# A gated linear-attention and MLP-mixer kernel: fewer idle products in batch 0, more engines for small copies, and a new written-out order

## The chip, the cores and the metric

The kernel runs on one core of a Trainium2 chip. A core has five engines that work side by side, each through its own instructions in their order: TensorE (PE in the profile, its weight loads PEld) for matrix products, VectorE (DVE), ScalarE (ACT) and GpSimd (POOL) for elementwise work, and SyncE (SP), which here only issues DMA transfers. Products land in PSUM, which this kernel uses as eight banks; everything else is in SBUF. An instruction waits on semaphores for what other engines and transfers make. The metric is the device time of one execution in microseconds (us), the median of several.

## The reference

Four batches, eight heads, 768 positions, 48 channels a head. First a linear attention with a forget gate, then an MLP mixer over its output:

```
f = 1 / (1 + exp(-f_logit))
for t in range(S):
    state = f[:, :, t, :, None] * state + einsum('bhd,bhe->bhde', k[:, :, t], v[:, :, t])
    y[:, :, t] = einsum('bhd,bhde->bhe', q[:, :, t], state)
x  = y as (B, S, H*D)
h  = max(x^T @ w_tok1, 0) @ w_tok2          # over positions: 768 -> 256 -> 768
u  = x + h^T
out = u + max(u @ w_ch1, 0) @ w_ch2         # over channels: 384 -> 1536 -> 384
```

## The kernel before

**Attention.** Each batch is cut into six chunks of 128 positions. For a chunk, `gates` makes the log gate on ACT (an exp, a log) and splits it into two bf16 parts; the lower part, Llo, is a subtraction (L457). `sums_and_turns` adds the gates up along the chunk with products by a triangle (L530 and L531; in chunk 5 of batch 0 one fp32 product, L519), takes exp of the sums on ACT (GG, L541 and L543), multiplies q and k by it on DVE (qk, L562) and transposes both. In batches 0 to 2 PE transposes (L579) and the results are copied from PSUM (qkT); in batch 3 a DMA transpose on SP does it (L569). `attention` then has the scores (L476) and the chunk's part of the state (L492). `rest` masks the scores on DVE (AmT, L616), decays the state (L625 to L633), copies it, rounded to bf16, into the two halves of a block-diagonal tile (state_bd, made at L636, the copy itself at L430, L432 or L434 by engine), and forms the output of the chunk from the state (L651) and the masked scores (L658). The output is copied from PSUM to x_bf, in bf16, and to x_nat. In batches 1 to 3 the decay of a chunk travels through a small DMA (glast from ends, L556).

**Mixer.** `mixer` has for each batch the first token product (tok1, L693, 12 products), a relu (h1T), the second (tok2, L709, 12), the addition of x (L725), a rounding to u_bf (L735), a transpose to uT (PE at L750 in batches 0 and 1, a DMA transpose in 2 and 3), the first channel product (L768, 24 groups of three), 24 relus to zT (ACT at L439 or DVE at L441), the second (L787, three groups of four for each of six row blocks, the last block in two column parts), the addition (L793) and a DMA to the output (L797).

**Order.** Nothing is left to a scheduler. Every step is an `Op` with the engines it may run on, what it needs and makes, and at most one PSUM bank. `ORDER` is a tuple of 1,116 codes, one for each step: `code // 4` says which step comes next, `code % 4` which of its engines takes it. Hence each engine's instructions stand in the order of the tuple, and an engine that waits holds up all that stands behind it. `Plan.best` walks through the tuple with estimated costs. Its estimated times pick the PSUM bank of each step and the place of **idle products**: where PE is estimated free for over 250 ns before `until` (25,500 ns), it puts in products of a constant tile (`steady`, L834) that nobody reads. `cold` is the time up to which the estimate counts every PE step twice.

**Loads.** POOL issues all loads but those of batch 0's gates (ACT and SP), one at a time, on one queue: k, q and v of a chunk of batch 0, then w_tok1, the last v, w_tok2, the channel weights, and the later batches' tiles. x_nat has three buffers, so batch 3 writes into that of batch 0 once its outputs have left.

The lines on which the change bears, beside the tuple:

```
n = int((t - free[PE] - 1000) / 430) if not free[PE] else min(4, int((t - free[PE]) / 220))
...
on = (DVE, DVE, (DVE, POOL), POOL)[b]                       # Llo, by batch
...
op = add(((ACT, DVE), ACT, (ACT, POOL), POOL)[b], r, None,  # state_bd, by batch
...
op = add((ACT,) if b <= 1 else (ACT, POOL), r, None,        # u_bf
```

Of the kernel before, what the change touches and what calls it, by code (L numbers as in the profile page):

```python
# [82 lines left out]
)  # L83
KEPT = 3
SPLIT = 5
SLOTS = (5110, 5800, 7500, 8450, 9600, 10400, 11400, 13000, 14400, 14800, 16700,
         18000, 19100, 19500, 20000, 20700, 21400, 23400, 24300, 25900)
HELD = (2600, 3600, 4100, 4750, 5500, 6500)


class Op:
# [18 lines left out]
class Plan:  # L110
# [65 lines left out]
    def best(self, idle, cold, until):  # L176
# [10 lines left out]
        for code in ORDER:  # L187
            op = self.ops[code // 4]
# [65 lines left out]
def kernel(  # L254
# [581 lines left out]
    for op in plan.best(idle, 6500.0, 25500.0):  # L836
        op.fn()
# [30 lines left out]
```

## Time and profile before

| | us |
|---|---|
| median of 3 runs | 172.84 |
| lowest and highest | 172.21, 174.68 |
| the profiled execution | 171.88 |
| its span, first to last instruction | 170.2 |
| PE busy, of it | 162.9 |
| DVE busy | 128.0 |
| ACT busy | 108.2 |
| POOL busy | 99.3 |

The profile is of one execution. A row of its timeline gives the start in us from the span's start, the length, the engine, the line, the operation with what it writes and reads, and in brackets the idle time before it with what ended it. Rows of groups give the busy time, the mean length in ns, and the idle time before. The chain of waits lists, in order of time, what released what, back from the last instruction. Products overlap in PE's pipeline, and the ends that the profile gives them are modelled: a row of eight products is shorter than eight lengths, and a PE shown as busy may still have short pauses.

### The profile page before, as it was taken

The page shows a single profiled execution, that of the slowest core. Times are in us where ns is not written, and L with a number is a line of the kernel's source. Part 1 is how long each engine was busy: PE and PEld are TensorE (multiplying, and loading weights), DVE is VectorE, ACT ScalarE, POOL GpSimd, SP SyncE. Part 2 cuts the span into 40 slices and gives each one's busy share as a digit, 9 for nine tenths or more (in the row PEclk, how much of TensorE's full clock was granted, in tenths as well). Part 3 has the DMA queues.
Part 4 walks back from the last instruction along what each step waited for, and adds up shares of the span by engine and source line. Part 5 has one row for each costly group of instructions (what it writes and reads, how often), then busy time and mean ns, then how long its engine had stood idle before and what let it go on. Part 6 is the DMA issues. An engine that isn't in the chain of part 4 may idle for free.

```text
span 170.2 us, 4181 instructions
## 1 busy us (share of the span) xinstructions
PE 162.9 (96%) x1606; PEld 102.8 (60%) x1606; DVE 128.0 (75%) x287; ACT 108.2 (64%) x256; POOL 99.3 (58%) x134
## 2 busy tenths in 40 slices
PE   6899999999999999999999999999999999999992
PEld 2356565665766576665776756665666666566661
DVE  5679995966898998899999868768884723675431
ACT  4759993598879889999999978385545320510100
POOL 7999569896499969999978869603111200000000
PEclk9999999999999999999999999999999999999999
DMA  6999999999999997999998999996920060220253
GB/s 103 141 174 149 156 192 181 212 149 201 192 167 136 161 165 75 116 155 133 182 157 49 134 251 107 144 165 115 228 100 4 0 139 0 92 96 0 78 202 139
DMA packets 102547, 22.71 MB, mean 133 GB/s; under 512 B 95264, under 2 KB 101664, under 8 KB 102528
## 3 DMA queue, kind: packets, MB, share of 16 engines
q0 software_dynamic: 79440, 13.77, 101.8%
q1 hardware_dynamic: 22560, 8.59, 22.5%
q8 instruction: 12, 0.20, 0.5%
q10 hardware_dynamic: 528, 0.10, 0.3%
q14 instruction: 7, 0.06, 0.1%
HBM read 25.17 MB, written 4.72 MB: 176 GB/s over the span
## 4 chain that ended last, share of the span: by engine, by line
PE 64%; DMA 12%; DVE 7%; ACT 6%; POOL 6%; issue 2%; SPq 1%; DVEq 0%; POOLq 0%
PE ps L768 22%; PE ps L787 22%; DMA v_sb<-in_v_dram 5%; PE ps L709 4%; POOL qk_sb L360 4%; PE ps L693 4%; DMA glast<-ends 4%; DMA out_dram<-x_nat 3%; DVE AmT L616 2%; PE ps L476 2%; PE ps L579 2%; PE ps L658 2%; POOL v_sb L360 1%; PE ps L530 1%; PE ps L651 1%
## 5 line engine op out<-in xcount | busy, mean ns | idle before, releaser
L787 PE MATMUL ps<-w_ch,zT 128*128 128x384 bf16 (+2 forms) x300 | 51.6, 320 | 0.0
L768 PE MATMUL ps<-uT,w_ch 128*128 128x384 bf16 x288 | 50.6, 326 | 0.0
L439 ACT ACTIVATE zT<-ps 128x384 bf16<-128x384 f32 x56 | 25.3, 494 | 25.3 <-PE ps L768 25.2
L768 PEld LDWEIGHTS <-w_ch 128*128 128x128 bf16 x288 | 27.7, 98 | 17.7
L787 PEld LDWEIGHTS <-zT 128*128 128x128 bf16 x300 | 27.9, 98 | 16.9
L616 DVE TENSOR_TENSOR AmT<-ps,tri_bf 128x512 bf16<-128x512 f32 x46 | 30.5, 686 | 2.5 <-PE ps L476 2.3
L441 DVE TENSOR_SCALAR zT<-ps 128x384 bf16<-128x384 f32 x40 | 21.1, 554 | 8.8 <-PE ps L768 8.8
L360 POOL DMA_DIRECT2D v_sb<-in_v_dram x24 | 22.2, 925 | 4.1 <-DMA w_ch<-in_moe_w_ch_dram 4.1
L360 POOL DMA_DIRECT2D qk_sb<-in_k_dram x24 | 22.4, 932 | 0.8 <-POOLq L852 0.8
L360 POOL DMA_DIRECT2D qk_sb<-in_q_dram x24 | 22.3, 930 | 0.0
L793 DVE TENSOR_TENSOR x_nat<-x_nat,ps 128x384 f32<-128x384 f32 (+2 forms) x25 | 13.3, 535 | 10.6 <-PE ps L787 10.2
L360 POOL DMA_DIRECT2D f_sb<-in_f_logit_dram x18 | 16.5, 943 | 0.2
L562 DVE TENSOR_TENSOR qk<-qk_sb,GG 128x768 bf16<-128x768 bf16 (+1 forms) x30 | 14.2, 475 | 2.1 <-ACT GG L543 1.0
L450 ACT ACTIVATE f_sb<-f_sb 128x384 f32<-128x384 f32 x24 | 12.5, 524 | 4.6 <-DMA f_sb<-in_f_logit_dram 4.4
L434 POOL CAST state_bd<-state 48x192 bf16<-48x192 f32 x13 | 4.5, 347 | 16.2 <-DVE state L633 14.6
L725 DVE TENSOR_TENSOR x_nat<-x_nat,ps 128x384 f32<-128x384 f32 x21 | 10.5, 550 | 3.4 <-PE ps L709 3.1
L834 PE MATMUL ps<-steady 128*128 128x512 bf16 x30 | 11.3, 483 | 1.7 <-DVE steady L375 1.7
L543 ACT ACTIVATE GG<-ps 128x384 bf16<-128x384 f32 x24 | 11.6, 489 | 2.0 <-PE ps L531 1.9
L541 ACT ACTIVATE GG<-ps 128x384 bf16<-128x384 f32 x24 | 11.7, 488 | 1.4 <-PE ps L531 1.2
L579 PE MATMUL ps<-ident,qk 128*128 128x128 bf16 x144 | 11.6, 224 | 0.0
L579 PEld LDWEIGHTS <-qk 128*128 128x128 bf16 x144 | 9.2, 100 | 2.7 <-DVE qk L562 0.7
L550 ACT ACTIVATE ends<-ps 32x384 f32<-32x384 f32 x15 | 7.0, 481 | 4.9 <-PE ps L531 4.7
(81 smaller groups left out, 234.1 us busy)
## 6 DMA issues: line engine op xcount, KB each, us to landing
out_dram<-x_nat SPq DMA_DIRECT2D x23, 192.0 KB, 3.1
f_sb<-in_f_logit_dram POOLq DMA_DIRECT2D x18, 192.0 KB, 5.4
qk_sb<-in_k_dram POOLq DMA_DIRECT2D x24, 96.0 KB, 5.1
qk_sb<-in_q_dram POOLq DMA_DIRECT2D x24, 96.0 KB, 4.9
v_sb<-in_v_dram POOLq DMA_DIRECT2D x24, 96.0 KB, 5.5
w_ch<-in_moe_w_ch_dram POOLq DMA_DIRECT2D x2, 576.0 KB, 7.5
w_ch<-in_moe_w_ch_dram POOLq DMA_DIRECT2D x1, 1152.0 KB, 10.6
f_sb<-in_f_logit_dram SPq DMA_DIRECT2D x5, 192.0 KB, 4.7
```

Of the source, the lines that this page charges most:

```text
L360: lambda eng=eng, into=into, of=of: eng.dma_start(out=into, in_=of),
L439: nc.scalar.activation(out_, in_, AF.Relu, bias=0.0, scale=1.0)
L441: nc.vector.tensor_scalar(out_, in_, 0.0, None, ALU.max)
L450: add(ACT, r, lambda: nc.scalar.activation(fb, fb, AF.Exp, bias=0.0, scale=-1.0), make=[key], kind=el, need=([("fb", c)] if c < 1 else []) ...
L541: add(ACT, r, lambda: nc.scalar.activation(G[i], sview(), AF.Exp, bias=0.0, scale=-1.0), make=[("G", i)], bank=p_s, kind=el)
L543: add(ACT, r, lambda: nc.scalar.activation(Gi[i], sview(), AF.Exp, bias=0.0, scale=1.0), make=[("Gi", i)], bank=p_s, kind=el)
L562: add(DVE, r, lambda n=n: nc.vector.tensor_tensor(qk[i4][:, n, :, 0:D], qk_sb[nb][:, n, :, c, :], GG[i][:, n], ALU.mult), need=[(x, nb, c) ...
L579: nc.tensor.transpose(to[:, o + hp, :], blk(src)[:, hp, :], ident)
L616: add(DVE, r, lambda half=half, made=made: nc.vector.tensor_tensor(half, made(), tb4, ALU.mult), need=["tri_bf"], make=[("AmT", i, p)], ba ...
L768: nc.tensor.matmul(banks[pm.at][:, 0:384], lhsT=w[:, kt, c0:c0 + 128], rhs=uT[:, th, :, kt, :], start=(kt == 0), stop=(kt == 2))
L787: nc.tensor.matmul(banks[pm.at][:, 0:n1 - n0], lhsT=zT[:, kt, tt * 128:(tt + 1) * 128], rhs=w_ch2[:, kt, n0:n1], start=(kt == 0), stop=(kt ...
L793: add(DVE, rank("ch2", tt), lambda un=un, pm=pm, n=n1 - n0: nc.vector.tensor_tensor(un, un, banks[pm.at][:, 0:n], ALU.add), make=[("x_nat" ...
```

## The change

Five edits, and a new tuple:

```
-                n = int((t - free[PE] - 1000) / 430) if not free[PE] else min(4, int((t - free[PE]) / 220))
+                n = int((t - free[PE] - 1000) / 430) if not free[PE] else min(4, int((t - free[PE]) / (430 if t < cold else 220)))
...
-        on = (DVE, DVE, (DVE, POOL), POOL)[b]
+        on = (DVE, (DVE, POOL), (DVE, POOL), POOL)[b]
...
-                op = add(((ACT, DVE), ACT, (ACT, POOL), POOL)[b], r, None,
+                op = add(((ACT, DVE), (ACT, POOL, DVE), (ACT, POOL, DVE), (POOL, ACT))[b], r, None,
...
-            op = add((ACT,) if b <= 1 else (ACT, POOL), r, None,
+            op = add((ACT, POOL), r, None,
...
-    for op in plan.best(idle, 6500.0, 25500.0):
+    for op in plan.best(idle, 10000.0, 25500.0):
```

Before 10,000 ns of estimated time, not 6,500, PE steps count double, and up to there one idle product is put in for each 430 ns of estimated pause, not 220. Llo and u_bf of batch 1 may now go to POOL; state_bd may go to POOL or DVE in batches 1 and 2, and to ACT in batch 3. All 1,116 steps are the same ones, and none is added or taken away but idle products.

What the built program makes of it: 19 idle products in place of 30. Seven stand at the start as before. Until the scores of chunk 1 the order on PE (without the products by ones, which give the chunk's decay) is

```
before: 7 idle, sums 0, 1 idle, sums 1, turn q0, 2 idle, state part 0, turn k0, 4 idle, scores 0,
        3 idle, sums 2, turn 1, state part 1, turn 1, output 0, 1 idle, turn 2, 2 idle, scores 1
after:  7 idle, sums 0, sums 1, turn k0, turn q0, state part 0, turn k1, scores 0, sums 2, turn q1,
        3 idle, output 0, 1 idle, scores 1
```

and from there the other eight idle products stand in runs of 1, 1, 4 and 2, the last run between the scores of chunk 5 and the first token product. On POOL the loads keep their order up to the channel weights. On SP the output DMAs of batch 0 and the transposes of batch 3 stand in another sequence, with the transposes of chunks 4 and 5 still ahead of the last two outputs of batch 0. From the second token product of batch 0 on, the steps on PE are the same products; most groups stand within 1 us of PE work of where they stood, and some groups of the second channel product 4 to 12 us away.

The engine of a step differs in these groups:

| step | from, to | how many |
|---|---|---|
| state_bd, batch 0 | ACT to DVE 2, DVE to ACT 1 | 3 |
| state_bd, batches 1 to 3 | ACT to DVE 3, ACT to POOL 1, POOL to ACT 4 | 8 |
| x_bf and x_nat from PSUM | DVE to ACT 8, ACT to DVE 3 | 11 |
| zT | DVE to ACT 24, ACT to DVE 22 | 46 |
| u_bf, batches 2 and 3 | ACT to POOL 5, POOL to ACT 4 | 9 |
| qkT, x_bf from x_nat, u_bf and uT of batch 0, h1T | both ways | 16 |

Llo and u_bf of batch 1 stay where they were (DVE and ACT).

120 rows, old and new, of the table ORDER are left out of this document.

## The prediction

> **What bounds the kernel now.** I read the page's engine shares first, then the windows of 10 us, because the stages differ. TensorE (PE) is the engine that is never free: after the first stage each window shows it busy for 9.6 us or more of 10, while VectorE (DVE) is its only neighbour that comes close, and only up to 90 us.
>
> ```profile
> span 170.2 us, 4181 instructions
> ...
> PE 162.9 (96%) x1606; PEld 102.8 (60%) x1606; DVE 128.0 (75%) x287; ACT 108.2 (64%) x256; POOL 99.3 (58%) x134
> ```
>
> ```profile
> 10.00:20.00 10.00, 9.67 (x137) 5.68 (x135) 9.86 (x26) 7.33 (x21) 8.53 (x11) 1.00 2.36 151
> ...
> 50.00:60.00 10.00, 9.61 (x118) 6.56 (x117) 9.20 (x22) 9.08 (x22) 10.00 (x13) 1.00 2.02 154
> ...
> 80.00:90.00 10.00, 10.00 (x136) 7.15 (x134) 9.60 (x21) 9.87 (x26) 8.41 (x11) 1.00 1.86 175
> ```
>
> The columns after the length are PE, its weight loads, DVE, ACT and POOL, then the granted clock and the DMA share. But a busy PE is not a useful PE here. The windows of the idle products alone (L834) show where it only kept itself busy:
>
> ```profile
> 0.00:5.00 5.00, 3.17 (x7) 0.88 (x7) 1.00 0.93 107
> 5.00:10.00 5.00, 1.95 (x4) 0.66 (x5) 1.00 1.96 160
> 10.00:15.00 5.00, 3.03 (x10) 0.76 (x8) 1.00 2.33 155
> 15.00:20.00 5.00, 1.58 (x5) 0.45 (x5) 1.00 2.38 146
> 20.00:25.00 5.00, 1.22 (x5) 0.41 (x5) 1.00 1.61 187
> ```
>
> So some 11 us of the first 25 are idle products, and the question for the change is whether they were in the way. The chain of waits says mostly not. Batch 0 waits for what arrives:
>
> ```profile
> 11.54 8.27 DMA v_sb<-in_v_dram
> ...
> 19.85 0.31 PE ps L492 x8
> ...
> 20.81 0.80 PE ps L519 x2
> ...
> 26.56 0.20 PE ps L658 x8
> 26.76 1.16 PE ps L693 x7
> ...
> 27.94 0.50 ACT h1T L439
> ...
> 28.48 1.22 PE ps L709 x6
> ```
>
> The v chunk issued at 11.54 lands at 19.81. All later loads of batch 0 are on the same queue, and GpSimd (POOL) issues them in the same order after the change. The last v chunk and w_tok2 close the stage, and the tiles' own answers (the second view lists issues between 16 and 21 us) give their delays:
>
> ```profile
> 17.54 0.99 POOL L360 DMA_DIRECT2D v_sb<-in_v_dram  x1
> 20.09 0.70 POOL L367 DMA_DIRECT2D w_tok<-in_moe_w_tok_dram  x1 [1.57 <-DMA v_sb<-in_v_dram]
> ```
>
> ```profile
> w_tok<-in_moe_w_tok_dram POOLq DMA_DIRECT2D x2, 384.0 KB, 7.5
> v_sb<-in_v_dram POOLq DMA_DIRECT2D x2, 96.0 KB, 7.3
> ```
>
> v of chunk 5 is there at about 17.54 + 7.3 = 24.8, w_tok2 at about 20.09 + 7.5 = 27.6. Token product 2 started at 28.48. **Ceiling of the first stage: 28.48 - 27.6 = 0.9 us.**
>
> From there on the ceiling is the work itself. One pace of each kind of product, from the chain, where PE runs without a wait:
>
> ```profile
> 32.22 7.80 PE ps L768 x48
> ...
> 72.54 0.38 PE ps L750 x6
> ...
> 75.04 0.55 PE ps L476 x16
> 75.60 0.36 PE ps L492 x16
> ...
> 77.38 0.17 PE ps L530
> 77.55 0.16 PE ps L531
> ...
> 81.97 0.17 PE ps L651 x4
> 82.14 0.40 PE ps L658 x16
> ...
> 83.36 0.89 PE ps L579 x16
> ...
> 166.87 0.26 DVE x_nat L793
> ```
>
> What is left at 28.48: products of 384 columns, 288 + 288 in the channel MLP, 48 in tok2, 36 in tok1 of batches 1 to 3, together 660 at 7.80/48 = 0.1625: 107.3. Eighteen chunks' gate sums at 0.33: 5.9. Their outputs, 15 x 0.17 + 18 x 0.20: 6.2. Scores, 9 x 0.55: 5.0. State parts, 7.5 x 0.36: 2.7. q and k transposes of batches 1 and 2, 6 x 0.89: 5.3. u transposes, 36 x 0.063: 2.3. Sum 134.7. It took 166.87 - 28.48 = 138.4, so all stalls after the first stage come to about 3.7 us, though the busy column hides most of them. **No order can gain more than 0.9 + 3.7 = 4.6 us.**
>
> **The change part by part.** Idle products. The built order has 19 in place of 30; the seven at the start stay, and the other 12 stand later (first a run of 3, behind the gate sums of chunk 2). Gone are above all the seven between 6 and 11 us, six of them here:
>
> ```profile
> 8.01 1.06 PE L834 MATMUL ps<-steady 128*128 128x512 bf16 x2
> ...
> 9.74 1.50 PE L834 MATMUL ps<-steady 128*128 128x512 bf16 x4
> 11.17 0.40 PE L476 MATMUL ps<-qkT 48*128 48x128 bf16 x8
> 11.50 0.82 PE L834 MATMUL ps<-steady 128*128 128x512 bf16 x3
> ```
>
> Scores of chunk 0 (L476 at 11.17) stood behind the run of four; without it they come up to 1.5 us earlier. That is worth nothing by itself: chunk 3 waits for v at 19.81 and chunk 5's gate sums (L519) start at 20.81, both set by loads. These products also did something: four cover 1.50 us at 9.74, three 0.82 us at 11.50, so a product's pace went from about 0.4 to about 0.22 us there. The granted clock column says 1.00 on both sides and does not show it. What their absence does to that step is the slow rival below.
>
> Order at the end of batch 0. The part products of chunk 3 (L492, at 19.85 in the old order) now stand behind L519, so they move from 19.85 to about 20.81 + 0.80 + 0.37 (outputs of chunk 2) = 22.0. Behind them wait the decay on DVE and two state copies, about 0.36 + 0.66, so 23.0, for the outputs of chunk 4 (before those of chunk 5 at 26.39): covered by 3 us. What ended the stage was DVE:
>
> ```profile
> 22.81 0.55 DVE L432 COPY x_nat<-ps 128x384 f32<-128x384 f32 x1
> ...
> 24.75 1.29 DVE L616 TENSOR_TENSOR AmT<-ps,tri_bf 128x512 bf16<-128x512 f32 x2
> ```
>
> The two masks of chunk 5 end at 26.04, and its outputs follow. The new order gives the x_nat copy at 22.81 to ScalarE (ACT) and leaves the rest of DVE's row there much as it was, so the pair of 1.29 can start up to 0.55 earlier. The tok1 tail (1.16), h1T (0.50) and tok2 follow as they did. I take **-0.6**; bounds 0 (the score chain of chunk 5 still hangs on L519) and -0.9.
>
> Engine choices. Of the state copies in batches 1 to 3, three go from ACT to DVE, one from ACT to POOL and four from POOL to ACT; the roundings of batch 1 stay on ACT and its Llo on DVE, so those freedoms are unused. Over all, DVE gives ACT eight copies of PSUM outputs and takes back three.
>
> ```profile
> L430 ACT ACTIVATE state_bd<-state 48x192 bf16<-48x192 f32 x17 | 6.1, 358 | 0.6 <-DVE state L633 0.3
> ...
> L434 POOL CAST state_bd<-state 48x192 bf16<-48x192 f32 x13 | 4.5, 347 | 16.2 <-DVE state L633 14.6
> ```
>
> One copy costs 0.36 on ACT and 0.35 on POOL, so the swap is even in work. On POOL it is a wait for DVE with loads queued behind (16.2 us of idle before 13 copies); the one new POOL copy, of batch 1 chunk 2, holds a v load and the two Llo subtractions of batch 2. Its price is bounded by a swap, 0, and one decay step more in PE's way, about 0.4. Four copies fewer there free the loads and Llo of batch 3 in the same measure. I take 0 for both.
>
> Order of batches 1 to 3. In PE's order most groups move by under 1 us of PE work; the largest moves are channel products 2, which have slack. I credit a small part of the 3.7 us of stalls, **-0.3**, bounds -3.7 and +1, since DVE at 9.20 and 9.60 of 10 sets part of them and it becomes only some 2 us lighter in 128. SP: the out-DMAs of batch 0, which x_nat of batch 3 waits for, keep their place near the transposes of batch 3. Nothing credited.
>
> Sum: -0.6 - 0.3 = -0.9 against the profiled execution's 171.88 (span 170.2), so 171.0. The median of the three runs shown is 172.84, 0.96 above it; on that footing **171.9**.
>
> **The rivals.** *The array stays slow (slower).* Between 6 and 11 us PE has only the work of chunks 0 and 1, at pauses; if the step from 0.4 to 0.22 needs gapless work, it comes later, and idle products, now counted at the fast pace after 10 us, take twice as long too. PE waits again for L519 from about 18 to 20.8, with four idle products in front. If the array is slow until the u transposes of batch 0, then tok1 and tok2 (24 x 0.1625) and 18 u transposes (18 x 0.063) cost 5.0 us more, less the 0.9 gained: 172.84 + 4.1 = 176.9. If dense work from 20.8 on wakes it by 25, only a backlog of about two chunks' products stays, each near 0.45 + 0.55/2 + 0.17 + 0.20 + 0.18 = 1.3: +2.6 - 0.9, 174.5. The point that decides is whether it is fast by about 21 us. For it: PE paced slowly for 9 us although busy 5.1 of the first 10 us with idle products alone. Against: the run of three from about 11.5 on, and that chunks 0 to 2 have time to spare before 19.8. [...]
>
> *Nothing reaches the end.* DVE sets batches 1 and 2, and an earlier tok2 waits there again: 172.8. For it: 9.2 to 9.9 of 10 busy up to 90 us.
>
> *The stalls go (faster).* The new order meets most of the 3.7 us besides the first stage: -0.9 - 2.9 = -3.8, 169.0. Against it: the dense DVE windows.
>
> **The numbers.** Forecast, 170.8 to 172.8: 0.46. Nothing reaches the end: 0.12. Slow array: 0.25, 0.20 of it near its full price and 0.05 at the 174.5 of an early waking. Stalls go: 0.17, of which 0.16 at or below its price. About 2%, or 3.5 us, is what a measurement of this kernel can tell from no change: slower begins at 176.3, faster at 169.4. So faster 0.16, slower 0.20, within 0.64. The range takes in the prices of both ends, 169.0 and 176.9, which leaves out about half of each end's chance; the forecast's own range is 170.8 to 172.8.
>
> **What would show it.** Right: L834 x19; tok2 (first L709) at about 27.9; L658 of chunk 5 before 26.2; the last L787 near 166. Wrong: idle products of 0.4 us after 12 us, or L768 at over 0.2 a piece (slow array); PE idle at L530 or L651 by more than 0.5 (a new wait); the first L709 after 28.5.

## The result, and the profile after

The changed kernel takes 173.91 us (median of 21 runs, 172.86 to 179.14) against 172.48 us for the kernel before, measured beside it (21 runs, 171.03 to 176.29). The ratio is 1.0098, 95% interval 1.0077 to 1.0118: 1.7 us slower, where 0.9 us faster was forecast. Ratios, here and below, are of the executions within 1.5% of the fastest of their kernel, the times are medians of all, so a ratio need not be that of the two medians. The profiled execution took 173.56.

The page's shares, after, show an engine that did less and a span that grew:

```profile
span 171.9 us, 4146 instructions
...
PE 161.2 (94%) x1592; PEld 102.1 (59%) x1595; DVE 127.2 (74%) x284; ACT 111.5 (65%) x261; POOL 99.7 (58%) x132
```

PE is busy 1.7 us less in a span 1.7 us longer, so it idles 3.4 us more. The windows say where. After, all engines, columns as in the prediction:

```profile
0.00:10.00 10.00, 6.67 (x43) 2.92 (x43) 5.82 (x27) 5.61 (x12) 8.80 (x18) 1.00 1.48 133
...
110.00:120.00 10.00, 8.38 (x68) 5.15 (x67) 6.98 (x16) 5.51 (x13) 3.69 (x7) 1.00 1.03 159
```

The same windows before:

```profile
0.00:10.00 10.00, 7.85 (x47) 3.42 (x48) 5.56 (x28) 6.34 (x14) 8.79 (x18) 1.00 1.45 133
...
110.00:120.00 10.00, 10.00 (x106) 6.29 (x105) 7.51 (x16) 6.48 (x15) 2.24 (x5) 1.00 1.09 141
```

The 1.2 us missing in the first window are idle products left out (1.95 us of them between 5 and 10 before, none after, below), no loss by itself. The 1.6 us missing between 110 and 120 are the loss: PE was full there before. The chain of waits of after, in that stretch (start, length, what):

```profile
117.77 0.50 ACT zT L439
...
118.28 0.56 DVE qk L562
118.84 0.48 DVE zT L441
...
119.36 1.14 PE ps L768 x6
```

The channel products of batch 2 stop for PSUM: the next bank comes free with a relu (zT) on DVE, and that relu stands behind a qk product. Why the qk product is late is told by POOL's and DVE's timelines of after:

```profile
108.96 1.61 POOL L457 TENSOR_TENSOR Llo<-f_sb 128x384 bf16<-128x384 f32 x2 [3.60 <-ACT f_sb L452]
110.64 0.73 POOL L434 CAST state_bd<-state 48x192 bf16<-48x192 f32 x2
111.31 0.92 POOL L360 DMA_DIRECT2D qk_sb<-in_k_dram  x1
112.23 0.88 POOL L360 DMA_DIRECT2D qk_sb<-in_q_dram  x1
...
118.28 0.56 DVE L562 TENSOR_TENSOR qk<-qk_sb,GG 128x768 bf16<-128x768 bf16 x1 [1.92 <-ACT zT L439]
118.76 1.48 DVE L441 TENSOR_SCALAR zT<-ps 128x384 bf16<-128x384 f32 x3
```

and of before:

```profile
105.37 0.89 POOL L360 DMA_DIRECT2D qk_sb<-in_k_dram  x1
106.24 0.90 POOL L360 DMA_DIRECT2D qk_sb<-in_q_dram  x1
107.13 1.65 POOL L457 TENSOR_TENSOR Llo<-f_sb 128x384 bf16<-128x384 f32 x2
...
115.67 0.55 DVE L562 TENSOR_TENSOR qk<-qk_sb,GG 128x768 bf16<-128x768 bf16 x1
```

The last loads of k and q in the kernel, those of batch 3's chunk 5, stood ahead of two Llo subtractions on POOL. The new order puts them behind these and behind two state copies. The subtractions wait 3.60 us for ACT and take 1.61, the copies take 0.73, and q is issued 6.0 us later (112.23 against 106.24). It lands at 118.09 against 114.02. The trace names ACT as what the qk product waited for, but the product reads q and the gates, not a relu; of what it reads, q came last (118.09, and the product starts at 118.28). That the load is the cause is shown by the runs below. The page's group of channel products carries the price: 1.8 us of idle where before it had 0.0.

```profile
L768 PE MATMUL ps<-uT,w_ch 128*128 128x384 bf16 x288 | 51.0, 326 | 1.8 <-DVE zT L441 1.6
```

The second difference is at the start. The windows of the idle products alone (L834), after:

```profile
5.00:10.00 5.00, 0.00 (x0) 0.00 (x0) 1.00 2.06 163
10.00:15.00 5.00, 1.61 (x3) 0.53 (x4) 1.00 2.30 157
```

Three products in 1.61 us between 10 and 15, where before ten took 3.03: the array is still slow there. The timeline of after has its step and the end of the first stage:

```profile
10.63 0.61 PE L476 MATMUL ps<-qkT 48*128 48x128 bf16 x8
...
12.85 1.06 PE L834 MATMUL ps<-steady 128*128 128x512 bf16 x2 [0.22 <-issue]
...
14.54 0.40 PE L476 MATMUL ps<-qkT 48*128 48x128 bf16 x8
...
20.70 0.72 DVE L432 CAST state_bd<-ps 48x192 bf16<-48x192 f32 x2
...
22.75 0.35 DVE L625 TENSOR_TENSOR ps<-ps,glast 128x192 f32<-128x192 f32 x1
23.02 0.62 DVE L562 TENSOR_TENSOR qk<-qk_sb,GG 128x384 bf16<-128x384 bf16 x1
...
25.45 1.28 DVE L616 TENSOR_TENSOR AmT<-ps,tri_bf 128x512 bf16<-128x512 f32 x2
...
26.74 0.39 PE L658 MATMUL ps<-v_sb,AmT 128*128 128x48 bf16 x8
...
28.76 0.97 PE L709 MATMUL ps<-h1T,w_tok 128*128 128x384 bf16 x5 [0.32 <-DVE h1T L441]
```

The eight score products at 10.63 took 0.61 us, those at 14.54, after the step, 0.40. The first product of tok2 starts at 28.76, 0.28 later than before.

### The profile page after: what moved, and what is told of

Same layout as the page of the kernel before. It is cut to its first block, busy times and chain, and to the rows that moved or that the text cites. A ratio compares the mean times of both kernels' runs of the same rounds, so it can differ in the third digit from the quotient of the medians.

```text
span 171.9 us, 4146 instructions
## 1 busy us (share of the span) xinstructions
PE 161.2 (94%) x1592; PEld 102.1 (59%) x1595; DVE 127.2 (74%) x284; ACT 111.5 (65%) x261; POOL 99.7 (58%) x132
## 4 chain that ended last, share of the span: by engine, by line
PE 78%; DMA 7%; ACT 6%; DVE 4%; issue 1%; POOL 1%; SPq 0%; DVEq 0%
PE ps L787 27%; PE ps L768 27%; DMA w_ch<-in_moe_w_ch_dram 4%; PE ps L579 4%; PE ps L693 3%; PE ps L476 3%; DMA f_sb<-in_f_logit_dram 3%; PE ps L530 2%; PE ps L658 2%; PE ps L709 2%; PE ps L531 2%; PE ps L492 2%; PE ps L651 2%; DVE qk L562 1%; DVE AmT L616 1%
## 5 line engine op out<-in xcount | busy, mean ns | idle before, releaser
L768 PE MATMUL ps<-uT,w_ch 128*128 128x384 bf16 x288 | 51.0, 326 | 1.8 <-DVE zT L441 1.6
L787 PE MATMUL ps<-w_ch,zT 128*128 128x384 bf16 (+2 forms) x300 | 51.6, 319 | 0.0
L439 ACT ACTIVATE zT<-ps 128x384 bf16<-128x384 f32 x58 | 26.9, 493 | 23.2 <-PE ps L768 22.8
L768 PEld LDWEIGHTS <-w_ch 128*128 128x128 bf16 x288 | 27.3, 98 | 19.2 <-issue 1.9
L787 PEld LDWEIGHTS <-zT 128*128 128x128 bf16 x300 | 28.1, 98 | 17.1
L441 DVE TENSOR_SCALAR zT<-ps 128x384 bf16<-128x384 f32 x38 | 19.7, 551 | 9.5 <-PE ps L768 9.4
L793 DVE TENSOR_TENSOR x_nat<-x_nat,ps 128x384 f32<-128x384 f32 (+2 forms) x25 | 12.9, 533 | 12.3 <-PE ps L787 12.1
L562 DVE TENSOR_TENSOR qk<-qk_sb,GG 128x768 bf16<-128x768 bf16 (+1 forms) x30 | 14.7, 503 | 4.6 <-ACT zT L439 1.9
L579 PE MATMUL ps<-ident,qk 128*128 128x128 bf16 x144 | 12.4, 230 | 0.9 <-DVE qk L562 0.7
L434 POOL CAST state_bd<-state 48x192 bf16<-48x192 f32 x10 | 3.6, 356 | 15.3 <-DVE state L633 13.4
L430 ACT ACTIVATE x_nat<-ps 128x384 f32<-128x384 f32 x19 | 9.3, 492 | 1.8 <-PE ps L709 0.8
L693 PE MATMUL ps<-x_bf,w_tok 128*128 128x384 bf16 x48 | 10.3, 325 | 0.0
```

The source lines that it names most:

```text
L439: nc.scalar.activation(out_, in_, AF.Relu, bias=0.0, scale=1.0)
L441: nc.vector.tensor_scalar(out_, in_, 0.0, None, ALU.max)
L562: add(DVE, r, lambda n=n: nc.vector.tensor_tensor(qk[i4][:, n, :, 0:D], qk_sb[nb][:, n, :, c, :], GG[i][:, n], ALU.mult), need=[(x, nb, c) ...
L579: nc.tensor.transpose(to[:, o + hp, :], blk(src)[:, hp, :], ident)
L693: add(PE, rank("tok1", rt), lambda rt=rt, kt=kt, pm=pm: nc.tensor.matmul(banks[pm.at][:, 0:DM], lhsT=w_tok1[:, kt, rt * 128:(rt + 1) * 128 ...
L768: nc.tensor.matmul(banks[pm.at][:, 0:384], lhsT=w[:, kt, c0:c0 + 128], rhs=uT[:, th, :, kt, :], start=(kt == 0), stop=(kt == 2))
```

## The experiments

Each ratio is against the kernel before, run beside it on the same chip, with its 95% interval. Numbers in a diff are codes of the order; 2048 and 2052 are the k and q loads, 3564 and 3660 the Llo subtraction and a state copy of batch 3, 3912 the qk product of chunk 5, 3293 the third relu behind it.

| kernel | idle products | us | ratio | interval |
|---|---|---|---|---|
| changed | 19 | 173.91 | 1.0098 | 1.0077 to 1.0118 |
| e1 | 19 | 171.64 | 0.9992 | 0.9958 to 1.0026 |
| e2 | 19 | 171.78 | 0.9985 | 0.9960 to 1.0009 |
| e3 | 30 | 172.72 | 1.0005 | 0.9967 to 1.0042 |
| e4 | 22 | 172.91 | 1.0059 | 1.0029 to 1.0090 |
| e5 | 25 | 173.94 | 1.0078 | 1.0034 to 1.0123 |
| e6 | 25 | 171.81 | 0.9956 | 0.9915 to 0.9997 |
| e8 | 30 | 171.65 | 0.9949 | 0.9913 to 0.9985 |
| e10 | 19 | 183.53 | 1.0625 | 1.0566 to 1.0685 |
| e11 | 19 | 182.72 | 1.0599 | 1.0538 to 1.0660 |
| e12 | 19 | 171.68 | 0.9994 | 0.9963 to 1.0024 |
| e13 | 7 | 173.08 | 1.0018 | 0.9977 to 1.0060 |
| e14 | 7 | 172.96 | 1.0023 | 0.9983 to 1.0064 |
| e15 | 25 | 171.83 | 0.9970 | 0.9932 to 1.0008 |
| e17 | 44 | 173.54 | 1.0101 | 1.0055 to 1.0147 |
| e18 | 52 | 174.56 | 1.0159 | 1.0113 to 1.0206 |

**The late loads.** e1 is the changed kernel with only the two loads ahead again; e2 leaves them late and lets the relus go first; e3 makes the loads late in the kernel before.

```
e1
-    3564, 3900, 3688, 3648, 3552, 3868, 3872, 3880, 3668, 3680, 2480, 2500, 2540, 3664, 3660, 3704, 2048, 3248,
+    2048, 2052, 3564, 3900, 3688, 3648, 3552, 3868, 3872, 3880, 3668, 3680, 2480, 2500, 2540, 3664, 3660, 3704,
...
-    2052, 3912, 3213, 3288,
+    3912, 3213, 3288,
e2
-    2052, 3912, 3213, 3288, 3264, 3256, 3261, 3268, 3244, 3312, 3316, 3696, 3772, 2524, 3293, 1380,
+    2052, 3213, 3288, 3264, 3256, 3261, 3268, 3244, 3312, 3316, 3696, 3772, 2524, 3293, 3912, 1380,
e3, in the order before: 2048 and 2052 taken out and put behind 3660
```

> The changed kernel with one edit: on GpSimd the last k and q loads of batch 3 (chunk 5) stand ahead of the two Llo subtractions and two state copies again, as in the kernel before. Theory A (late loads: the q load lands at 118.1, VectorE's qk product waits for it, a relu to zT stands behind that product, and TensorE has no free bank): the 1.8 us pause of TensorE at L768 near 117 falls below 0.3, and the time falls by 1.3 to 1.8 us, a ratio to the kernel before of 0.999 to 1.003. Theory B (the array gets fast later in batch 0, for want of idle products): pause and ratio stay, 1.008 to 1.012. Theory C (the order of batches 1 to 3 as a whole is worse, the pause only shows it): the pause goes, but others of the same sum open, ratio above 1.005.

> The changed kernel with the loads left late and one edit on VectorE: the three relus to zT that stood behind the qk product of batch 3 chunk 5 stand ahead of it. Theory A: the q load still lands near 118, but TensorE no longer waits for it; the pause at L768 near 117 falls below 0.6 and the time by 1.0 to 1.8 us, ratio 0.999 to 1.005. If ScalarE's relus were the cause (the profile names ScalarE as what ended VectorE's wait), the pause stays and the ratio too. Theory B: no change.

> The kernel before with the opposite edit: the same k and q loads are moved behind the two Llo subtractions and the two state copies on GpSimd; banks and all else as they were. Theory A: the loads are issued at about 111 instead of 105.4 and 106.2, the q load lands near 117.5, the qk product that ran at 115.7 slips by some 2 us, and relus stand behind it: TensorE pauses by 0.5 to 1.8 us there, ratio 1.002 to 1.010. Theory B and C: no change, 0.998 to 1.002.

Both mendings take the pause away and about 1% with it. POOL's and DVE's timelines of e1:

```profile
106.51 0.92 POOL L360 DMA_DIRECT2D qk_sb<-in_k_dram  x1
107.42 0.88 POOL L360 DMA_DIRECT2D qk_sb<-in_q_dram  x1
110.18 1.61 POOL L457 TENSOR_TENSOR Llo<-f_sb 128x384 bf16<-128x384 f32 x2 [1.88 <-ACT f_sb L452]
...
117.48 0.55 DVE L562 TENSOR_TENSOR qk<-qk_sb,GG 128x768 bf16<-128x768 bf16 x1
```

No wait stands before the qk product any more, and the group of channel products of e1 shows what is left of its idle time, from another cause:

```profile
L768 PE MATMUL ps<-uT,w_ch 128*128 128x384 bf16 x288 | 51.0, 326 | 0.2 <-DMA w_ch<-in_moe_w_ch_dram 0.2
```

In e2 the loads are as late as in the changed kernel (q issued at 112.30, landed at 118.51; the product starts at 118.70) and it costs nothing: the 36 channel products from 112.76 to 118.77 run without a pause. e3 fell short of its expectation: in the old order DVE came to the qk product at 116.5, q landed at 116.74, the product waited only 0.30 us and the time did not move. So the same late issue was nearly covered there. A late load alone is not the loss; the loss is a late load with relus queued behind the product that waits for it.

**The idle products.** Three kernels change the number of idle products in the two kernels compared: e4 has the new rule in the old order (PSUM banks as before), e5 the old rule in the changed kernel (with `cold` the estimate changes, so its banks may differ), e13 the old order with the first seven alone.

```
e4, e12, and the changed kernel: cold is 10000.0, and for a pause, n is
    min(4, int((t - free[PE]) / (430 if t < cold else 220)))
e5, e6, e8, e15, and the kernel before: cold is 6500.0, and n is
    min(4, int((t - free[PE]) / 220))
e13, e14: n is 0
e17, e18: n is
    min(8, int((t - free[PE]) / 130))
```

e6 is the changed kernel with the edits of e1 and e2 together and the old rule; e15 is e6 once more. e12, e14 and e17 change the rule in e6 (e12 with each PSUM bank as in e6). e8 and e18 have the first 202 steps of the old order, up to the second token product of batch 0, and then the new order as in e6.

> The kernel before, order, banks and engines untouched, with the new rule for idle products alone: 22 instead of 30, nine fewer between 6 and 12 us. Theory B: products keep the slow pace (0.43 us for 512 columns) past 10.9 us, to about 14 us or later; the first second token product starts 0.2 to 1.0 us later than 28.5; ratio 1.001 to 1.006. Theory A: whatever the pace does early is hidden by the loads, 0.998 to 1.001.

> The changed kernel with the old rule for idle products (25 of them in place of 19; every other step in the same order). Theory B (fewer idle products let the array step to its fast pace some 3.4 us later, and that costs about 1 us beside the 1.8 us pause): the array is fast by about 11 us, the first second-token product (L709) starts 0.3 to 1 us earlier than 28.76, the pause of 1.8 us near 117 stays, ratio to the kernel before 1.003 to 1.007. Rival A alone (the late k and q loads are the whole loss, idle products are worth nothing): no different from the changed kernel, 1.008 to 1.011, wherever the array's step falls.

> The changed kernel with the k and q loads of batch 3's chunk 5 ahead of the two Llo subtractions, the three relus ahead of the qk product that waits for them, and the old rule for idle products (25). If both losses are real and add up: the pause near 117 is gone, the array is fast by about 11 us, ratio 0.992 to 0.997. If idle products are worth nothing: 0.998 to 1.000, as with either edit of the loads alone.

> Batch 0 in the old order and with the old 30 idle products, then from the second token product of batch 0 on the new order and engines, with the loads and relus of batch 3 mended as in the run beside it. If the new order of batches 1 to 3 is worth something of the 3.7 us of pauses: 0.994 to 0.998. If it is worth nothing once mended: 1.000. Against the run with the new order of batch 0 and 25 idle products it tells what the new batch 0 is worth: nothing if the two agree within 0.3%.

> The kernel with both mendings of batch 3 (loads and relus) with the new rule's 19 idle products, and every PSUM bank as in its sister with 25. Theory B: the array steps up some 3 us later than in the sister, ratio 0.998 to 1.001 against the sister's 0.9956. Rival (idle products worth nothing): 0.9956 within 0.2%.

> The kernel before with only the seven idle products at the start in place of 30. Theory B (each pause that is left empty puts the array's step off): the array is slow until 14 us or later, the first second-token product (L709) is at 29 or later, ratio 1.006 to 1.03. Rival (idle products worth nothing, batch 0 waits for loads): 0.998 to 1.002.

> The kernel with both mendings and only the seven idle products at the start in place of 25; every other step as in the sister. Theory B: ratio 1.003 or more, the array slow past 14 us. Rival (idle products worth nothing): 0.9956 within 0.2%.

> The kernel with both mendings of batch 3 and 25 idle products once more, beside the next two on one chip. Theory B: 0.993 to 0.998. If its earlier ratio was a lucky chip: 0.998 to 1.001, as its sister with 19.

> The same kernel with 44 idle products: each estimated pause of PE over 250 ns up to 25.5 us is filled with one per 130 ns, at most eight. [...]

> The old order of batch 0 with 52 idle products in place of 30, then the new order of batches 1 to 3 with both mendings. Theory B: no fall of the granted clock, 0.992 to 0.996. Rival (idle products stand in the way): above 0.998.

e4 cost 0.6%, clear of no change. In the mended new order, 44, 25, 19 and 7 idle products gave 1.0101, 0.9956 and 0.9970, 0.9994, 1.0023: both ends are worse than the middle. The step from 25 to 19 is 0.2 to 0.4% in each of the pairs (e5 with the changed kernel, e6 and e15 with e12), always of one sign and always within its interval. Not all came as expected. e5 was to start tok2 0.3 to 1 us earlier and to come to 1.003 to 1.007; its tok2 started at 28.8, as in the changed kernel, and 1.0078 lies between its two expectations. e13 was to come to 1.006 or more and came to 1.0018, with an interval that reaches from below no change to e4's own value; e14, at 1.0023, is just short of its 1.003. That fewer products cost some 0.2 to 0.6% is what the runs together say; a size for each product they don't give.

Too many are as bad. e17 was expected at or below the ratio of 25 if idle products help, 0.3% or more above it if they stand in the way of work, e18 at 0.992 to 0.996. The granted clock shows no fall in them, as expected (1.00 in every window of 5 us up to 30), but they are 1.0 and 1.6% slower than the kernel before. The profile of e18, with 52, says how; its timeline of PE at the end of the first stage:

```profile
27.88 1.03 PE L834 MATMUL ps<-steady 128*128 128x512 bf16 x4 [0.16 <-issue]
...
30.14 1.46 PE L693 MATMUL ps<-x_bf,w_tok 128*128 128x384 bf16 x8
32.02 1.30 PE L709 MATMUL ps<-h1T,w_tok 128*128 128x384 bf16 x7 [0.42 <-ACT h1T L439]
```

The array is fast there (the four idle products at 27.88 take 1.03 us, four in the kernel before 1.50 at 9.74), w_tok2 has landed at 28.21 and v's last chunk at 26.34, and still tok2 starts at 32.02, against 28.48 in the kernel before, whose batch 0 has the same order. Of its chain of waits between 15 and 34 us, 29.5% is L834: the products stand in the way of the chunks' own. How the array's pace falls and rises, which the granted clock shows in some of these kernels, is told in the last section.

**The engines of the state copies.** e10 is e2 with the eight state copies of batches 1 to 3 back on their old engines. e11 is e2 with only the four back that went from POOL to ACT, each PSUM bank kept as in e2.

```
e11
-  2716, 2900, 3849, 3957
+  2717, 2901, 3848, 3956
e10, these and
-  1670, 1781, 2714, 3014
+  1668, 1780, 2712, 3012
```

> The changed kernel with the three relus ahead of the qk product (the pause near 117 gone) and the eight small state copies of batches 1 to 3 back on the engines they had before; 19 idle products. If the free choice of engine is worth nothing, as predicted: within 0.2% of the same kernel with the new engines (0.9985), so 0.997 to 1.001. If the copies' engines carry a gain that the pause hid: 1.003 or more.

> The changed kernel with the three relus ahead of the qk product, and only the four state copies that went from POOL to ACT back on POOL (two in batch 2, two in batch 3), at their places in the new order and with every PSUM bank as it was. Theory P (a copy's place in POOL's queue is the price: it stands behind up to eight load issues of some 0.9 us each, and PE waits for it): PE pauses of 2 us and more at L651 near 84 and 138 as in the run with all eight copies back, total 8 to 11 us above the same kernel with the copies on ACT, ratio 1.045 to 1.065. Rival Q (the 10 us of that run came from the other four copies or from its other PSUM banks): under 2 us, ratio below 1.011. The prediction's price, even in work: 0.9985.

e10 was expected to change nothing and took 11 us more than e2 (1.0625 against 0.9985). Since its PSUM banks differ from e2's, e11 repeats the core of it with the banks held: 1.0599, against 0.9985 for the same kernel with these four copies on ACT. That is the size which the queue was expected to cost; the pause came at L768, not at L651. The timelines of e11, POOL, DVE and PE:

```profile
82.40 1.10 POOL L360 DMA_DIRECT2D v_sb<-in_v_dram  x1
83.27 1.12 POOL L360 DMA_DIRECT2D f_sb<-in_f_logit_dram  x1
84.44 0.34 POOL L434 CAST state_bd<-state 48x192 bf16<-48x192 f32 x1
...
84.81 0.36 DVE L633 TENSOR_TENSOR state<-tsum,glast 128x192 f32<-128x192 f32 x1 [5.60 <-POOL state_bd L434]
85.09 0.55 DVE L441 TENSOR_SCALAR zT<-ps 128x384 bf16<-128x384 f32 x1
...
85.69 1.12 PE L768 MATMUL ps<-uT,w_ch 128*128 128x384 bf16 x3 [4.87 <-DVE zT L441]
```

A copy of 0.34 us stands behind eight load issues that began at 77.19. DVE waits 5.60 us before it may overwrite the state, the relus wait behind that, and PE waits 4.87 for a bank. It is the pause of 117 once more, in larger. But the pause is only about half of the 10.6 us. After it the array was slow, too: the granted clock reads 0.50 from 84.56 to 91.39, and three products of 384 columns that take 0.65 us at 80.17 take 1.12 at 85.69. An estimate from that: 6.8 us at half pace lose up to 3.4. Two pauses near 138, at L651 for a copy on POOL (0.58) and at L658 for v (1.65), make up most of the rest.

## Why the prediction was wrong, point by point

**Engine choices, "I take 0 for both": this is the step that failed.** The prediction said of POOL: "Four copies fewer there free the loads and Llo of batch 3 in the same measure." It counted copies and did not put POOL's queue of batch 3 beside the new one. The wait it had wrong is that of DVE for these loads: they were to come earlier, and the new order has them behind Llo and two copies, q is issued 6.0 us later, and PE stands 1.8 us. It is the order on POOL that delays them; the term for the order looked at PE, DVE and SP. The three kernels that mend it and keep 19 idle products (e1, e2, e12) average 0.9990; the changed kernel's 1.0098 is 1.08% above, 1.9 us of 172.5. So this one pause is as large as the whole slowdown, and with it alone mended the kernel is level with the one before. Nor is the swap of copies even, as taken from their lengths (0.36 and 0.35): in the new order, four copies on POOL cost 10.6 us (1.0599 against 0.9985), by where they stand in its queue and by the slow stretch that followed the pause (granted clock 0.50 for 6.8 us).

**First stage, -0.6: failed, with little weight.** "What ended the stage was DVE" was not what the chain of waits before said. The masks ended at 26.04, and by the timeline the L658 of chunk 5 followed at 26.39; in between PE was busy, with work that runs on from 24.21 and has three idle products in it. The chain before:

```profile
24.61 0.75 PE ps L834 x3
25.37 0.65 PE ps L693 x4
```

Nor did "leaves the rest of DVE's row there much as it was" hold. Two state copies of batch 0 came to DVE (0.72 at 20.70), and the decay of chunk 3, behind L519 now, stands at 22.75 ahead of the last qk product of chunk 5. The pair of masks starts at 25.45, 0.70 later, not up to 0.55 earlier; tok2 at 28.76, not 27.9. They end at 26.73, and the outputs start at 26.74, when PE, busy since 25.34, comes to them: no wait for the masks shows here either. The landings, estimated from medians, were 25.30 before and 25.52 after for v's last chunk (24.8 in the estimate) and 27.15 and 27.82 for w_tok2 (27.6), each about a microsecond ahead of its first product. In time the new batch 0 is worth nothing that these runs can tell from noise: e8 (old batch 0) has 0.9949, e6 and e15 (new batch 0) 0.9956 and 0.9970.

**Order of batches 1 to 3, -0.3: the sign was right and the size too small.** The gain is there once the loads are mended: e8, which has batch 0 as before, is 0.5% faster than the kernel before (0.9949, interval below 1), 0.9 us. That is order and engines together; only the state copies were parted from it (e10, e11). As built, with the late loads, the term came to 1.9 - 0.9 = +1.0, at the end of its bounds and for a reason that they did not contain: POOL's queue in batch 3.

**The slow array: a real cost, at a fraction of its price.** Its test was idle products of 0.4 us after 12 us, and they are in the trace of after (two in 1.06 us at 12.85). Its step came at 14 us against 10.7, long before the 21 us from which the backlog was to count. That gapless, dense work brings the step, on which this rival and its 174.5 rested, was the author's supposition and is not shown: in e14 the granted clock stayed at 0.50 after 3.35 us of work in 3.45 (14.55 to 18.00). What fewer idle products cost is 0.2 to 0.6%, 0.3 to 1.0 us, not the 5.0 of the rival. By what path they cost it stays open: in e3 the array is fast from 4.6 us on, and its tok2 still starts at 29.1, later than the 28.48 of the kernel before.

**The sum again**, in ratios: mended order with 25 or 30 idle products 0.9949 to 0.9970, 19 in place of them about 0.3% more, the late loads 1.1% more: 1.009 to 1.011, against 1.0098 measured. The forecast's -0.9 is nearly what the order and engines give without the two losses, but by luck: -0.6 of it was to come from the first stage, which gave nothing. Of the tests, L834 x19 came true; tok2 after 28.5 and chunk 5's L658 at 26.74 said wrong in the first stage, and the last L787 ended at 168.3, not near 166. For a new wait the prediction looked at L530 and L651, and it came at L768, behind relus.

**What follows for the kernel:** with the loads mended and the old number of idle products it runs 0.3 to 0.5% faster than before (e8, e6, e15; the interval of e15 just reaches no change); no other run was faster. That the run-to-run spread of the landings (v's last chunk at 24.83 in e15, 26.37 in e3) sets part of what is left is argued from single profiles, not shown.

## What to carry to other kernels

An instruction that is moved or given to another engine is priced by what stands ahead of it and behind it in that engine's queue, not by its length: list each queue before and after, loads included, to the end of the kernel, and for each wait that arises ask who stands behind the waiter. A copy of 0.34 us cost PE a pause of 4.9 us in this way, and for 6.8 us after it the granted clock read 0.50; two loads of 0.9 us cost 1.8. When a rewritten order comes out slower, mend the one wait that the chain names before the rest is judged: here it hid a gain of 0.3 to 0.5%.

## What the hardware showed that had not been expected

The array's pace went down again within the first stage, in stretches of 3.4 us or two or five times that. The prediction noted that the granted clock stays at 1.00 over a step from slow to fast. In six of the other profiled runs the column does show it: the array was fast by 6 us (the gate sums of 384 columns at 0.17 each), then the clock fell to 0.50 (first between 7.8 and 8.5 us), and rose later. Of nine runs that were fast so early, the six that fell have 7 (e13, e14), 19 (e2, e10), 22 (e4) and 25 idle products (e5), the three that held 25 (e15) and 30 (e3, e8). In the first stage the array is fast to stay from 4.3 to 11.3 us on in the eight profiles with 25 or more, from 12.9 to 16.4 in the seven with 19 or 22, and from 24.8 and 25.2 in the two with seven (by the products' pace where the column does not show the rise). The windows of e4, cut at its fall and rise:

```profile
4.60:8.00 3.40, 2.14 (x25) 1.10 (x25) 2.54 (x14) 2.94 (x9) 3.40 (x6) 1.00 1.90 140
8.00:11.45 3.45, 2.78 (x31) 1.55 (x31) 2.54 (x8) 1.82 (x6) 3.45 (x6) 0.51 2.33 165
11.45:14.90 3.45, 3.45 (x37) 2.32 (x34) 3.14 (x9) 3.05 (x9) 3.45 (x6) 0.51 2.21 163
14.90:18.30 3.40, 3.40 (x59) 2.12 (x57) 2.92 (x8) 2.16 (x6) 3.06 (x5) 1.00 2.30 149
```

and of e14, with seven idle products:

```profile
4.35:7.75 3.40, 2.35 (x27) 1.06 (x26) 2.04 (x7) 2.57 (x6) 3.40 (x7) 1.00 1.98 143
...
14.55:18.00 3.45, 3.35 (x49) 2.47 (x47) 3.03 (x8) 3.22 (x8) 3.04 (x4) 0.50 2.19 151
...
21.40:24.85 3.45, 3.45 (x33) 2.54 (x34) 2.74 (x8) 2.35 (x7) 2.13 (x3) 0.50 1.62 189
```

The slow stretches last 3.4 us in e5, 6.8 or 6.9 in e2, e4 and e10, both lengths in e13, and 17.1 in e14: one, two and five times 3.42. Cut in such pieces, each of these falls follows one in which PE was busy for 2.0 to 2.4 us, and each rise after a fall one with 3.2 to 3.45; pieces with up to 3.35 in e14 did not raise it, so the busy time, which is modelled, does not tell by itself after which piece the clock rises. When the array becomes fast differs from one execution to the next: the same kernel was fast from 10.3 us on in the profile of e6 and by 5.7 in that of e15. A piece with less work than those ahead of the falls could hold the pace. The pause of the changed kernel, in a piece of this length that the author laid around it (the column shows no step there), and the one of e11, in a piece that ends at the fall, after and e11:

```profile
116.82:120.23 3.41, 1.79 (x12) 0.91 (x10) 1.95 (x4) 1.91 (x5) 0.00 (x0) 1.00 0.78 145
120.23:123.65 3.42, 3.42 (x49) 2.18 (x48) 2.79 (x7) 1.77 (x4) 0.69 (x2) 1.00 0.86 238
```

```profile
81.15:84.56 3.41, 0.00 (x0) 0.00 (x0) 0.00 (x0) 0.91 (x2) 3.37 (x5) 1.00 1.99 101
84.56:87.97 3.41, 2.28 (x22) 1.77 (x22) 3.16 (x8) 1.36 (x4) 2.96 (x5) 0.50 1.26 153
```

With 1.79 us of work and a pause of 1.62 the clock stayed at 1.00; after a piece with none at all it fell. What tells the 1.79 that held from the 2.0 to 2.4 that did not, no run here shows. So these runs give an idle product no price of its own. That its worth hung on where it fell in such a piece is the author's reading, not shown; that it can stand in the way is (29.5% of the chain of e18 between 15 and 34 us).

The granted clock column reads 1.00 until the first fall, even where the array is slow: in the kernel before, two products of 512 columns take 1.06 us at 8.01 (the second starts 0.43 after the first) and three take 0.82 at 11.50 (0.22 apart), at 1.00 both times. So in these profiles a column of 1.00 at the start was no sign of a fast array; the products' pace was.
